# Letting the second part's experts go some 20 items into the third group's 48-point stage instead of at the end of the sort

## The chip, the cores and the metric

The kernel runs on one core of a Trainium2 chip. The metric is the device time of one execution in microseconds. Before the change it is 2397.02 us, the median of three runs (2395.26 to 2405.26).

## What is computed

A causal convolution along the sequence, by FFT in the reference, feeds a mixture of experts in which each token goes to one expert:

```python
L = 2 * S                                   # S = 5696, x: 8 x 5696 x 128
y = irfft(rfft(x, n=L) * rfft(h, n=L), n=L)[:, :S]
x = y.reshape(8 * 5696, 128)
expert_idx = argmax(x @ w_gate, axis=1)     # 8 experts
gate_w = softmax(x @ w_gate)[expert_idx]
for e in range(8):                          # w1[e]: 128 x 1024, w2[e]: 1024 x 128
    out[expert_idx == e] = gate_w * (relu(x @ w1[e]) @ w2[e])
```

## The kernel before

The eight sequences are split into three groups of 2, 3 and 3 (`SPLIT`), and each group has one part, which is the unit of sorting and of expert work. A group passes through these stages:

- `phase_a`: 119-point transforms of the input, stored to `U` in DRAM. For the third group it runs as a *guest* inside the second group's sort (class `Guest`), and its stores of `U` are at L271.
- `phase_b`: the 48-point stage. It has 120 items, one for each frequency `q`, in 30 blocks of 4. An item goes through: a cut of the input into a high and a low half (L488 on ScalarE, L490 on VectorE), three forward matmuls (L472, tile `xp`), two copies (L499, L500), a product on VectorE (L503) and one on GpSimd (L504), their sum on VectorE (L510), the inverse matmul (L518, tile `vp`), a save (L527), and a store to `V` (L563). For each block it loads `uq` from `U` (L418), `mi` (L421) and `hh` (L425) on SyncE's queue, and the forward matrices `mt` on GpSimd's queue (L407). It prefetches two blocks before its first item and further blocks two ahead.
- `phase_c`, called by `gather`: the last transform (L652), routing, and the sort. Each column of tokens is scattered to its expert's region of `SR` by an indirect DMA on GpSimd's queue (L589). What is left of them is put out at the end of `phase_c`, so all of them stand ahead of whatever GpSimd gets next. Then `tables` computes on VectorE which rows and which expert each tile of 256 tokens has, and notes the last eight scatters in `pt.ends`.
- `moe`: the experts. The second part has 67 tiles of four steps each. A step has six matmuls of layer 1 (L993), a ReLU on ScalarE (L999), its remainder on VectorE (L1001) and six matmuls of layer 2 (L1013). For each tile the rows `xr` are loaded on SyncE (L943, behind a read of the table at L941 and a wait for `pt.ends`), weights `wb` where the expert changes (L962), rows transposed on TensorE (tile `mx`), the result drained (L1023) and scattered by GpSimd (L1036).

The order of all instructions is written out by a planner, `run`, which draws on two streams, `experts()` and `rest()`. Each `yield` names a cost; a stream's clock advances by the cost over its share (1.0 for the experts, 0.75 for the rest), and the stream that is furthest behind writes its next instructions. This is the order in which every engine and every queue executes. `experts()` gives way as long as `pt.ready` of the next part is not set; when it is set, it takes the other stream's time. By these costs, the first part's 37 tiles end just as the second group's `phase_c` ends, and `rest()` goes on with the third group's `phase_b`, which yields 6000 once (`GAPS[1]`) and 998.4 for each item. The third group's `gather` follows.

Of the kernel before, what the change touches and what calls it, by code (L numbers as in the profile page):

```python
# [48 lines left out]
GAPS = (0, 6000, 5000)  # L49
HOLD = (0, 0, 0)  # L50
AHEAD = 2
A3 = (True, True, False)
ALO = ('gpsimd', 'vector', 'vector')
AT = 650
# [10 lines left out]
def conv_moe(ctx: ExitStack, tc: tile.TileContext, I, out, B, S, D, E, F, split):  # L65
# [68 lines left out]
    for g, nbs in enumerate(split):  # L134
        gr = Group(g, b0, sum(nbs))
# [104 lines left out]
    def steps_a(gr, tag, bufs):  # L240
# [7 lines left out]
        xts, uts, xss = {}, {}, {}  # L248
        split = A3[g]

# [56 lines left out]
    def phase_a(gr):  # L307
        start, begin, store, flush, M = steps_a(gr, "six", SIX)
        half = AT if gr.g == 0 else 750 * RATE[3 * gr.g - 3]
        start()  # L310
        for m in range(M + 2):
            if m < M:
                begin(m)
            yield half
            flush()
            if 1 <= m <= M:
                store(m - 1)
        yield 0
        flush()

    class Guest:
# [4 lines left out]
        def begin(self, count):  # L326
            if self.m == 0:
                self.start()
            for _ in range(min(count, self.M - self.m)):
                self.step(self.m)  # L330
                self.open.append(self.m)
                self.m += 1
# [6 lines left out]
        def rest(self):  # L339
            while self.m < self.M:  # L340
                self.begin(2)
                yield 1500 * RATE[3 * self.gr.g - 3]
                self.end()
            yield 0
            self.flush()
# [260 lines left out]
    def phase_c(pt, guest=None):  # L606
# [27 lines left out]
        def divide(n, k):  # L634
            if not pt.c3 or n >= nu:
                return
            src = vqs[n][:, :, k * cw : (k + 1) * cw]
            vr = sb.tile([QN, 2, 2, cw], F32R, tag="six", name=f"vr{g}_{n}_{k}", bufs=SIX)
            nc.scalar.copy(vr[:, 0], src)
            nc.vector.tensor_tensor(out=vr[:, 1], in0=src, in1=vr[:, 0].bitcast(F32), op=ALU.subtract)  # L640
            vrs[n, k] = vr
# [15 lines left out]
        def settle(n, k):  # L657
            if k == 0:
                rt = sb.tile([MP, NI, nb, RW], F32, tag="rt", name=f"rt{g}_{n}", bufs=6)
                nc.vector.tensor_tensor(  # L660
                    out=rt[:, :, :, D + 1].bitcast(I32),
                    in0=idb[:, pt.b0 : pt.b0 + nb].rearrange("p (o b) -> p o b", o=1).broadcast_to([MP, NI, nb]),
                    in1=ioff[:, n * NI : (n + 1) * NI].rearrange("p (i o) -> p i o", o=1).broadcast_to([MP, NI, nb]),
                    op=ALU.add,
                )
                rts[n] = rt.rearrange("p i b w -> p (i b) w")
            done = nc.scalar.copy(
                rts[n][:, k * cb : (k + 1) * cb, :D],
                ybank.pop((n, k))[:MP, :cw].rearrange("p (b d) -> p b d", d=D),
            )  # L670
            sort_one(done.ins)
# [127 lines left out]
        if gr.g:  # L799
            yield GAPS[2]  # L800
        for k in range(AHEAD):
            divide(*divmod(k, nsub))
# [4 lines left out]
        for n in range(n_end + 1):  # L807
            for k in range(nsub):
# [18 lines left out]
                if n < nu:  # L827
                    divide(*divmod(at + AHEAD, nsub))
                    settle(n, k)
# [84 lines left out]
    def fill(pt):  # L914
        g, base = pt.s, state["base"]
        dr = sb.tile([1, E], I32, tag="dr", name=f"dr{g}")
        nc.vector.tensor_copy(dr, base[0:1, :E])
        yield 20000
        for e in range(-1, E):
            row = E * CAP  # L920
            if e >= 0:
                row = nc.sync.value_load(dr[0:1, e : e + 1], min_val=0, max_val=E * CAP - T)
            s = nc.sync.dma_start(SR[ds(row, T), :].rearrange("(p s) w -> p s w", s=2), dummy).ins
            tc.declare_no_dep(s, group="sr", reason="rows past the last token of an expert")
            tc.add_to_no_dep_group("sr", s)
            pt.ends = pt.ends + [s]
            yield 2000
# [174 lines left out]
    def gather(pt, guest=None):  # L1102
        state["hold"] = HOLD[pt.s]
        yield from phase_c(pt, guest)
        state["hold"] = 0
        tables(pt)
        if pt is parts[-1]:
            yield from fill(pt)
        pt.ready = True
        yield 0  # L1110

    def chain(*gens):
# [2 lines left out]

    def rest():
        yield from phase_a(groups[1])
        for gr in groups[1:]:
            yield from phase_b(gr)
            guest = Guest(groups[gr.g + 1]) if gr.g + 1 < len(groups) else None  # L1120
            for pt in gr.parts:
                yield from gather(pt, guest)
            if guest:
                yield from guest.rest()

    def experts():
        for pt in parts:
            while not pt.ready:
                yield None
            yield from moe(pt)  # L1130
# [29 lines left out]
    with tc.manual_schedule():  # L1160
        prep = weights()
        back = rest()
        run((phase_a(g0), 1.0), (phase_h(), SHARES[4]), (consts(), 1.0), (prep, SHARES[5]), stop=(prep,))
        sb.close()
        sb.open("b")
        first = phase_b(g0)
        run((first, 1.0), (prep, SHARES[0]), until=first)
        sb.close()
        sb.close()
        sb.open("sb")  # L1170
        first = chain(*[gather(pt) for pt in g0.parts])
        run((first, 1.0), (prep, SHARES[1]), (back, SHARES[2]), until=first)
        run((prep, 1.0))
        lull = pause(LULL[0])
        run((lull, 1.0), (back, LULL[1]), until=lull)
        run((experts(), 1.0), (back, SHARES[3]))
        sb.close()
# [78 lines left out]
```

## Time and profile before

| | us |
|---|---|
| median of three runs | 2397.02 (2395.26 to 2405.26) |
| the profiled execution | 2403.89 |
| its span, first to last instruction | 2402.1 |
| mean granted TensorE clock | 0.945 |

| engine | busy us | share of the span |
|---|---|---|
| TensorE matmul (PE) | 2111.8 | 88% |
| TensorE weight load (PEld) | 1797.5 | 75% |
| VectorE (DVE) | 1599.4 | 67% |
| ScalarE (ACT) | 1453.6 | 61% |
| GpSimd (POOL) | 1236.6 | 51% |

A busy time is the union of an engine's instructions; issuing a DMA from SyncE does not count as busy, but SyncE's queue is served in order, so that an instruction that waits there holds up all behind it. The share is a mean over stages with different limits, so the stretch around the change has to be read by itself. In rows, "[38.16 <-DMA xr<-SR]" is the engine's idle time before the instruction and what ended it; "Lnnn" is a line of the kernel.

### The profile page before, as it was taken

Reading aid. Unit: us, or ns where it says so; the run is one execution under the profiler, and the core shown is the slowest. Engines: PE = TensorE matmul, PEld = TensorE weight load, DVE = VectorE, ACT = ScalarE, POOL = GpSimd, SP = SyncE. Lnnn points to the kernel's source line nnn. Section 1 sums busy time; section 2 is a strip of 40 time slices with the busy share of each in tenths; the row PEclk is TensorE's granted clock in tenths of the full one; section 3 lists DMA queues with packets and bytes.
Section 4 is the critical chain, followed back from the end, with each engine's and each line's share of the span. In section 5 each row is a group of like instructions: output and inputs, shape, how many; then the busy total and the mean of one; then the engine's idle time right before and its main releaser. Section 6 shows DMA issues by size and latency. Waiting matters only on the chain.

```text
span 2402.1 us, 48507 instructions
## 1 busy us (share of the span) xinstructions
PE 2111.8 (88%) x14238; PEld 1797.5 (75%) x14238; DVE 1599.4 (67%) x3807; ACT 1453.6 (61%) x3193; POOL 1236.6 (51%) x1281
## 2 busy tenths in 40 slices
PE   6888687659898899995689988999987899999998
PEld 4666454437677777774678777899877899999998
DVE  3578654559898746665599998767665455555554
ACT  3699653348888745552588887666543444444444
POOL 4487536725555427677355555457776223232323
PEclk8999898769999999997899999999998999999999
DMA  8999898699999678883898998566633222222221
GB/s 250 307 280 297 249 317 232 195 247 239 234 261 235 170 203 248 250 251 103 193 224 205 228 209 209 137 157 172 164 87 100 81 77 80 75 77 77 79 75 34
DMA packets 274473, 439.10 MB, mean 183 GB/s; under 512 B 32433, under 2 KB 200679, under 8 KB 274208
## 3 DMA queue, kind: packets, MB, share of 16 engines
q1 hardware_dynamic: 243552, 365.29, 56.7%
q0 software_dynamic: 30656, 70.69, 10.6%
q8 instruction: 116, 1.90, 0.3%
q14 instruction: 149, 1.22, 0.2%
HBM read 601.91 MB, written 166.06 MB: 320 GB/s over the span
## 4 chain that ended last, share of the span: by engine, by line
PE 48%; DMA 17%; issue 12%; DVE 7%; ACT 7%; POOL 4%; SPq 3%; POOLq 0%; DVEq 0%; ACTq 0%
PE mh L993 14%; PE ma L1013 14%; PE yp L652 5%; PE pa L278 4%; DMA wb<-WD 4%; DMA SR<-rt,pi 3%; DMA xt<-x 2%; PE vp L518 2%; PE mx L166 2%; DVE hs L1001 2%; DMA mi<-miq 2%; POOL out L1036 2%; PE tp L691 2%; PE xp L472 1%; ACT xs L500 1%
## 5 line engine op out<-in xcount | busy, mean ns | idle before, releaser
L993 PE MATMUL mh<-xtb,wb 128*128 128x256 f32 x4368 | 726.6, 302 | 79.5 <-DVE hs L1001 47.4
L1001 DVE SCALAR_TENSOR_TENSOR hs<-mh,hs 128x512 fp32r<-128x512 f32 x728 | 499.7, 686 | 411.4 <-ACT hs L999 410.9
L993 PEld LDWEIGHTS mh<-xtb,wb 128*128 128x128 f32 x4368 | 594.4, 192 | 184.4 <-DVE hs L1001 77.9
L999 ACT ACTIVATE hs<-mh 128x512 fp32r<-128x512 f32 x728 | 435.2, 598 | 460.8 <-PE mh L993 458.2
L1036 POOL DMA_INDIRECT out<-xr x364 | 369.8, 1016 | 638.0 <-DVE xr L1027 557.2
L1013 PE MATMUL ma<-hs,wb 128*128 128x256 f32 x4368 | 661.8, 288 | 10.0 <-DMA wb<-WD 9.8
L1013 PEld LDWEIGHTS ma<-hs,wb 128*128 128x128 f32 x4368 | 578.6, 192 | 13.8 <-DMA wb<-WD 13.1
L589 POOL DMA_INDIRECT SR<-rt,pi x384 | 394.0, 1026 | 214.4 <-issue 73.6
L504 POOL TENSOR_TENSOR xs<-xs,hh 128x384 f32<-128x384 f32 (+1 forms) x360 | 345.4, 971 | 255.9 <-ACT xs L500 221.9
L510 DVE TENSOR_TENSOR zt<-zt,xs 128x384 f32<-128x384 f32 (+1 forms) x300 | 293.0, 977 | 44.2 <-POOL xs L504 44.2
L518 PE MATMUL vp<-zt,mi 128*96 128x384 f32 (+1 forms) x720 | 274.7, 464 | 17.9 <-DVE vt L527 9.3
L472 PE MATMUL xp<-us,mt 96*128 96x384 f32 x720 | 193.4, 374 | 28.6 <-DVE us L490 14.5
L503 DVE TENSOR_TENSOR zt<-xp,hh 128x384 f32<-128x384 f32 (+1 forms) x360 | 180.8, 502 | 40.8 <-ACT xs L500 39.7
L499 ACT ACTIVATE xs<-xp 64x384 f32<-64x384 f32 (+1 forms) x360 | 162.8, 452 | 36.2 <-DVE zt L510 24.2
L488 ACT CAST us<-uq 96x384 fp32r<-96x384 f32 x240 | 123.2, 514 | 75.5 <-PE xp L472 57.2
L472 PEld LDWEIGHTS xp<-us,mt 96*128 96x128 f32 x720 | 124.6, 199 | 57.1 <-DVE us L490 24.8
L490 DVE TENSOR_TENSOR us<-uq,us 96x384 fp32r<-96x384 f32 x240 | 149.7, 625 | 22.9 <-ACT us L488 22.7
L500 ACT COPY xs<-xp 64x384 f32<-64x384 f32 (+1 forms) x360 | 156.6, 435 | 4.2
L518 PEld LDWEIGHTS vp<-zt,mi 128*96 128x96 f32 x720 | 111.9, 166 | 55.2 <-POOL xs L504 25.3
L278 PE MATMUL pa<-xc,fcr 120*120 120x512 f32 x360 | 115.1, 461 | 35.0 <-ACT ut L290 12.5
L527 ACT COPY vt<-vp 96x384 f32<-96x384 f32 x240 | 114.1, 476 | 11.2 <-PE vp L518 5.5
L278 PEld LDWEIGHTS pa<-xc,fcr 120*120 120x120 f32 x360 | 71.3, 212 | 62.9 <-ACT xc L256 13.5
(129 smaller groups left out, 2592.2 us busy)
## 6 DMA issues: line engine op xcount, KB each, us to landing
wb<-WD SPq DMA_DIRECT2D x728, 512.0 KB
vq<-V SPq DMA_DIRECT2D x64, 720.0 KB
U<-ut SPq DMA_DIRECT2D x48, 720.0 KB
uq<-U SPq DMA_DIRECT2D x60, 576.0 KB
V<-vt SPq DMA_DIRECT2D x60, 576.0 KB
xr<-SR SPq DMA_DIRECT2D x182, 130.0 KB
xt<-x SPq DMA_DIRECT2D x96, 240.0 KB
mt<-mqs POOLq DMA_DIRECT2D x60, 384.0 KB
```

The lines of the kernel that those rows point to most:

```text
L278: nc.tensor.matmul(banks[m][:QN, :], lhs, rhs, start=(k == 0), stop=(k == len(ops) - 1))
L472: nc.tensor.matmul(xp[:, :cw], mt[:, at + u, :], us[:, v], start=(k == 0), stop=(k == 2))
L503: nc.vector.tensor_tensor(out=zt, in0=x3, in1=hv[:, 0].broadcast_to([P, cb, D]), op=ALU.mult)
L504: nc.gpsimd.tensor_tensor(out=xs, in0=xs, in1=hv[:, 1].broadcast_to([P, cb, D]), op=ALU.mult)
L510: eng.tensor_tensor(out=zt, in0=zt, in1=xs, op=ALU.add)
L518: nc.tensor.matmul(vp[:K2, :cw], mi[:, k0, :], zt.rearrange("p b d -> p (b d)"), start=True, stop=True)
L589: s = nc.gpsimd.indirect_dma_start(out=SR[:, :], out_offset=IndirectOffsetOnAxis(ap=pi[:, b : b + 1], axis=0), in_=rt[:, b, :], in_offset= ...
L993: nc.tensor.matmul(hp[:, u, :], wb[:, a, f, :], xt[:, b, :], start=(n == 0), stop=(n == 2))
L999: done = nc.scalar.activation(hs[:, 0], hp, AF.Relu)
L1001: nc.vector.scalar_tensor_tensor(out=hs[:, 1], in0=hp, scalar=0.0, in1=hs[:, 0].bitcast(F32), op0=ALU.max, op1=ALU.subtract)
L1013: nc.tensor.matmul(accs[j], wb[:, a, f, :], hs[:, b, u, :], start=(k == 0 and u == 0 and n == 0), stop=(k == NPAIR - 1 and u == 1 and n == 2),
L1036: sc = nc.gpsimd.indirect_dma_start(out=out[:, :], out_offset=IndirectOffsetOnAxis(ap=xr[:, s, D + 1 : D + 2].bitcast(I32), axis=0), in_=x ...
```

## The change

A part whose sort has a guest is no longer marked ready at the end of its sort. `rest()` keeps it in a list and marks it ready when the next group's `phase_b` has spent more than `HEAD` of the planner's cost. Only the second part has a guest, so only its experts are concerned.

```diff
+HEAD = 26000
@@ gather
         if pt is parts[-1]:
             yield from fill(pt)
-        pt.ready = True
+        if guest is None:
+            pt.ready = True
         yield 0
@@ rest
         yield from phase_a(groups[1])
+        wait = []
         for gr in groups[1:]:
-            yield from phase_b(gr)
+            spent = 0
+            for cost in phase_b(gr):
+                spent += cost
+                yield cost
+                if spent > HEAD and wait:
+                    wait.pop().ready = True
             guest = Guest(groups[gr.g + 1]) if gr.g + 1 < len(groups) else None
             for pt in gr.parts:
                 yield from gather(pt, guest)
             if guest:
                 yield from guest.rest()
+                wait.append(gr.parts[-1])
```

## Rows read from the trace of the kernel before

**Rows 1.** The page's span in 40 slices: TensorE's busy tenths in each

```profile
PE   6888687659898899995689988999987899999998
```

**Rows 2.** Stretches: length, busy us (instructions) by engine, granted clock, DMA share, GB/s

```profile
core 0: us, PE busy (x) PEld busy (x) DVE busy (x) ACT busy (x) POOL busy (x), PEclk, DMA share, GB/s
1120.00:1140.00 20.00, 0.00 (x0) 0.00 (x0) 5.90 (x18) 0.00 (x0) 15.27 (x16) 0.50 0.17 48
1140.00:1160.00 20.00, 5.60 (x25) 4.97 (x26) 1.81 (x3) 1.86 (x4) 5.28 (x7) 0.51 0.83 229
...
1940.00:2380.00 440.00, 435.23 (x3633) 431.80 (x3632) 239.26 (x420) 211.24 (x420) 135.00 (x139) 1.00 0.25 75
```

**Rows 3.** Waits of SyncE's queue, 1085 to 1185: total us, times, longest us

```profile
SPq L943 <- DMA SR<-rt,pi: 20.6, 3, 17.8
SPq L941 <- DVE ej L895: 19.3, 1, 19.3
```

**Rows 4.** Timeline of GpSimd: start, us, line, operation, tiles, count, idle before

```profile
1143.59 0.99 POOL L589 DMA_INDIRECT SR<-rt,pi  x1 [0.31 <-issue]
1144.59 1.62 POOL L407 DMA_DIRECT2D mt<-mqs  x3
```

**Rows 5.** Timeline of SyncE's DMA issues in the same stretch

```profile
1101.86 3.89 SPq L271 DMA_DIRECT2D U<-ut  x2
1146.44 2.69 SPq L943 DMA_DIRECT2D xr<-SR  x3
1150.26 2.26 SPq L962 DMA_DIRECT2D wb<-WD  x4
...
1153.70 0.43 SPq L418 DMA_DIRECT2D uq<-U  x1
```

**Rows 6.** Timeline of TensorE: first expert matmuls, first item, item 22 (1233.09)

```profile
1153.07 0.66 PE L166 MATMUL mx_None<-ident,xr 128*128 128x128 f32 x2 [38.16 <-DMA xr<-SR]
1154.93 4.68 PE L993 MATMUL mh<-xtb,wb 128*128 128x256 f32 x18 [1.20 <-DMA wb<-WD]
...
1169.65 0.79 PE L472 MATMUL xp<-us,mt 96*128 96x384 f32 x3
...
1233.09 0.69 PE L472 MATMUL xp<-us,mt 96*128 96x384 f32 x3
```

**Rows 7.** Line 993 from 1154 to 1233.1: count, ns min/median/max, first and last start

```profile
L993 PE MATMUL mh<-xtb,wb x162: 277/282/582, 1154.9 to 1231.8; 128*128 128x256 f32 x162
```

**Rows 8.** Timeline at the second group's first items: SyncE and TensorE

```profile
477.32 10.73 SPq L271 DMA_DIRECT2D U<-ut  x4
513.58 2.67 SPq L943 DMA_DIRECT2D xr<-SR  x3
500.11 4.42 PE L472 MATMUL xp<-us,mt 96*128 96x384 f32 x10 [13.13 <-ACT us L488]
...
522.18 0.69 PE L166 MATMUL mx_None<-ident,xr 128*128 128x128 f32 x2 [5.50 <-DMA xr<-SR]
525.96 1.62 PE L993 MATMUL mh<-xtb,wb 128*128 128x256 f32 x6 [3.09 <-DMA wb<-WD]
```

**Rows 9.** Line 472 from 500 to 516

```profile
L472 PE MATMUL xp<-us,mt x27: 338/525/1095, 500.1 to 515.6; 96*128 96x384 f32 x27
```

**Rows 10.** VectorE's groups, 505 to 516: count, busy us, mean ns, idle before

```profile
L510 DVE TENSOR_TENSOR zt<-zt,xs 128x384 f32<-128x384 f32 x6 | 5.5, 910 | 0.0
L490 DVE TENSOR_TENSOR us<-uq,us 96x384 fp32r<-96x384 f32 x5 | 4.6, 915 | 0.0
L503 DVE TENSOR_TENSOR zt<-xp,hh 128x384 f32<-128x384 f32 x6 | 3.3, 545 | 0.1
```

**Rows 11.** Line 1023, one drain a tile, from 1940 to 2380

```profile
L1023 ACT COPY ot<-ma x70: 372/373/374, 1940.9 to 2375.9; 128x256 f32<-128x256 f32 x70
```

**Rows 12.** Waits of the engines, 1775 to 1850

```profile
DVE pi L784 <- DMA SR<-rt,pi: 6.6, 1, 6.6
```

**Rows 13.** Stretch after the restart in the second group's stage

```profile
525.00:530.00 5.00, 4.04 (x13) 3.37 (x14) 1.72 (x3) 1.57 (x4) 0.75 (x1) 0.50 1.03 401
```

## The prediction

> **What bounds the kernel now.** I read the page's forty slices first [rows 1]. TensorE is at 0.8 to 0.9 almost everywhere, with one hole in the nineteenth and twentieth slice, 1081 to 1201 us. The table of stretches [rows 2] places it: TensorE does nothing from 1120 to 1140, 5.60 us of work from 1140 to 1160, and in the last stretch, where only experts are left, 435.23 of 440 us. So the end is set by TensorE with expert tiles, and whatever is put off to the end is paid there at TensorE's full price.
>
> SyncE's waits tell what it did in the hole [rows 3]: its first instructions for the second part's experts stood 19.3 us for the table (L941) and 17.8 us at most for the sort's scatters (L943). The same wait is seen from GpSimd [rows 4]: the scatters (L589) go out one by one until 1143.59 + 0.99 us, and only behind them the third group's matrices `mt` (L407) at 1144.59. On SyncE [rows 5] the last store of `U` starts in the run at 1101.86, then nothing until the rows `xr` at 1146.44, the weights `wb` at 1150.26, and the third group's first `uq` at 1153.70, behind the experts. On TensorE [rows 6] the row transposes come at 1153.07 after 38.16 us idle, the first expert matmul at 1154.93, the first matmul of the 48-point stage (L472) at 1169.65.
>
> **What the change moves, by the code.** `HEAD` is 26000. `phase_b` of the third group yields 6000 once, then 0.78 x 384 x 8 / 2.4 = 998.4 an item; 6000 + 21 x 998.4 = 26966 is the first sum above it, and that resumption also writes out the next item. So 22 items (0 to 21) stand ahead of the second part's first expert instruction on every queue; before, the experts stood ahead of item 0. No instruction is added or removed, and no wait.
> - SyncE: the table reads, 3 `xr` and 4 `wb` loads move behind the loads of blocks 0 to 6 and the `V` stores of blocks 0 to 3. The last of these waits for item 15's save, so SyncE comes to the experts when TensorE is at about item 21.
> - GpSimd: nothing is moved past the scatters; `mt` still follows them. The experts' output scatters of the first tiles go later, onto a queue that is free then; I price that at nothing. Cover gone, it would be two instructions a tile of about 1 us each.
> - TensorE, VectorE, ScalarE: the first expert steps move behind 22 items. Their number is counted: when item 22's first matmul ran in the profile, at 1233.09 us [rows 6], 162 matmuls of layer 1 had started [rows 7], six to a step, 27 steps. After the change one step stands there. So 26 steps, 6.5 tiles, are put off.
>
> **The sum.** I compare the moment at which item 22 runs, since from there the interleaving is the same in both (0.75 against 1), and then add the 6.5 tiles that are still owed.
> 1. Start of the stage. `uq` can go as soon as `U` has landed and no longer waits for the experts, but the first matmul also needs `mt`, issued at 1144.59. How long `mt` takes to land isn't shown; the weights, 512 KB, went from issue to first use in 4.7 us (1150.26 to 1154.93), `mt` is 384 KB: I take 4.4, so 1149. Ends: 1147 and 1151. Of the hole, only its last 5 us are filled.
> 2. Items 0 to 21 alone. The profile has the same situation once: the second group's stage ran its first items alone just before the first part's experts [rows 8, 9]. Ten matmuls, over three items, took 4.42 us, so 1.4 us an item while the pipeline fills; 27 matmuls, nine items, started from 500.1 to 515.6. Steady, VectorE is full: 910 + 915 + 545 = 2370 ns an item [rows 10]. I take 4 x 1.4 + 17 x 2.3 = 44.7 us from item 0's start to item 21's, so 1193.7. Ends: (515.6 - 500.1) / 9 = 1.7 for all 21 (36 us), and the mixed pace (1233.09 - 1169.65) / 22 = 2.9 for the 17 (55 us).
> 3. The experts' start in mid-stage. TensorE takes its queue in order: the row transposes wait for `xr`, and the items behind them wait too. From SyncE's first `xr` to the first expert matmul it was 8.5 us in the hole (1146.44 to 1154.93) and 12.4 us in the earlier case (513.58 to 525.96, with 5.50 us idle ahead of the transposes and 3.09 for `wb`) [rows 8]. I take 11, as the earlier case has the same loads in flight: 1204.7. Item 22 follows its step by 1.4: 1206.1.
> 4. After that wait the granted clock was 0.50 for the 5 us after restart [rows 13]; that costs 2 us here (ends 0 and 5): 1208.1.
> So item 22 runs 1233.1 - 1208.1 = 25.0 us earlier. The 6.5 tiles owed run at the end among experts alone: 70 drains from 1940.9 to 2375.9 are 435.0 / 69 = 6.30 us a tile [rows 11], 41.0 us (at a tile per 7.6 us, as behind the second sort, it would be 49). Net 41.0 - 25.0 = **16 us slower**.
>
> The reason in a sentence: in the mixed stage TensorE works on experts while VectorE works on items, and the change takes 6.5 tiles out of that mixture, though the hole they were meant to leave is held open by GpSimd's queue.
>
> The second sort's end is also a weak place: VectorE waits 6.6 us for a scatter (L784) [rows 12]. After the change 18.5 instead of 12 tiles of the second part remain there by the planner's costs, but TensorE stood behind VectorE's queue, not without tiles; I price it at nothing, ends -4 and +4.
>
> The profiled execution took 2403.89 us (span 2402.1), 6.9 above the median of the runs, 2397.02. The sum gives 2419.9 for an execution like the profiled one, and 2413 for the median.
>
> **Rivals.**
> - *Faster: the items fill the hole.* Place: the first L472 matmul. If `mt` did not wait behind the scatters, item 0 would need only `uq`. Earlier it ran 12.1 us after the last `U` store's issue ended (477.32 + 10.73 = 488.05 to 500.11) [rows 8]; from 1101.86 + 3.89 = 1105.75 that gives 1118. Then item 22 runs at 1118 + 59.1 = 1177, 56 us earlier, net -15: 2382. It decides once the first matmul is ahead of 1233 - 41 - 59 = 1133. For it: SyncE is free from 1106. Against: `mt` came right behind the last scatter, and the diff changes nothing ahead of it on GpSimd. Chance 0.07. The Trainium skill speaks for this rival: its page "DMA: Bandwidth & Descriptors", section "Issuing engines are not separate DMA queues", says that transfers issued from different engines interleave on the same sixteen engines and that the issuing engine matters only for the sequencer's time, usually small. By that the wait on GpSimd would be minor and 2382 would come out; the row shows over 30 us of issuing ahead of `mt`, so I hold to the row.
> - *The experts' start is hidden.* If SyncE runs so far ahead that `xr` and `wb` are there when TensorE arrives, steps 3 and 4 cost nothing: item 22 at 1193.7 + 1.4 = 1195.1, 38 us earlier, net +3: 2400. For: SyncE prefetches three blocks. Against: it passes a `V` store that waits for item 15. Chance 0.13.
> - *The hold does nothing that counts,* because the tiles put off find idle TensorE time later (the 0.9 of the mixed stage, the second sort's end): net about 0, 2397. For: TensorE isn't full there. Against: the planner keeps the same ratio of experts to items. Chance 0.06.
>
> **How the numbers follow.** The forecast has 0.74; with its ends (item 22 at 1195 or at 1225, 6.30 to 7.6 us a tile) it spans about +2 to +36 us, and its lower fifth, 0.14, lies within 12 us of no change. A measurement of this kernel can tell about 0.5%, 12 us, from no change. Slower by more: 0.60. Within: 0.14 + 0.13 + 0.06 = 0.33. Faster: 0.07. The range 2398 to 2430 takes in the forecast but its outermost end, and the hidden start; it leaves out the first rival and about half of the third.
>
> **What would show it.** Right: first L472 matmul of the third group at 1147 to 1151, behind the last scatter and `mt`; about 2.3 us from item to item; then a gap of 5 to 9 us on TensorE at the row transposes; item 22 at about 1208; the second part's first expert matmul at about 1205 instead of 1154.93; tail tiles at 6.3 us and the last tile 16 us later. Wrong: an L472 matmul ahead of 1133; items alone at under 1.8 us; no gap at the transposes; or a mixed stage after item 22 whose pace differs from before.

## The result, and the profile after

The changed kernel took 2426.97 us (median of seven runs, 2421.22 to 2434.33); the kernel before, in seven runs beside them, 2397.02 (2393.15 to 2410.83). The ratio is 1.0126, with a 95% interval of 1.0104 to 1.0148: 30 us slower, where the forecast was 16 in a range of 1 to 33. The profiled execution of after took 2434.33 us (span 2432.5), 30.4 us of span more than the profiled one of before.

The slices and stretches of after, read as [rows 1, 2] (the first line is the page's row of slices; the others give length, busy time of each engine with its instructions, granted clock, DMA share, GB/s):

```profile
PE   7888697568998799993798898999968999999998
1120.00:1140.00 20.00, 0.00 (x0) 0.00 (x0) 6.73 (x20) 0.00 (x0) 15.42 (x16) 0.50 0.74 178
1140.00:1160.00 20.00, 9.66 (x23) 6.29 (x23) 8.34 (x12) 8.41 (x18) 10.96 (x13) 0.50 0.37 81
1160.00:1190.00 30.00, 24.07 (x72) 11.99 (x71) 30.00 (x43) 26.39 (x56) 16.97 (x17) 0.91 0.98 214
1940.00:2380.00 440.00, 433.44 (x3592) 429.70 (x3592) 236.46 (x414) 208.97 (x415) 134.24 (x139) 0.99 0.25 75
```

TensorE's hole from 1120 to 1140 is there as before, and the stage of experts alone is as full as before. In the stretch in which items now run alone, 1160 to 1190, it is VectorE that is busy for 30.00 of 30.00 us. The slices have a new dent, the "6" in the thirtieth, 1764 to 1824 us, where the third group's sort ends.

The start of the stage in the timelines of after (SyncE's issues, GpSimd, TensorE), the answer to [rows 4 to 6]:

```profile
1105.27 0.33 SPq L272 DMA_DIRECT2D U<-ut  x1
1110.50 0.33 SPq L419 DMA_DIRECT2D uq<-U  x1
1193.14 2.98 SPq L944 DMA_DIRECT2D xr<-SR  x3
...
1143.49 1.00 POOL L590 DMA_INDIRECT SR<-rt,pi  x1 [0.30 <-issue]
1144.47 1.65 POOL L408 DMA_DIRECT2D mt<-mqs  x3
...
1149.34 4.12 PE L473 MATMUL xp<-us,mt 96*128 96x384 f32 x10 [34.47 <-DMA mt<-mqs]
1198.75 0.69 PE L167 MATMUL mx_None<-ident,xr 128*128 128x128 f32 x2 [4.31 <-DMA xr<-SR]
1200.68 1.62 PE L994 MATMUL mh<-xtb,wb 128*128 128x256 f32 x6 [1.24 <-DMA wb<-WD]
1202.10 1.16 PE L473 MATMUL xp<-us,mt 96*128 96x384 f32 x3
```

SyncE fetched the first `uq` at 1110.50, 43 us earlier than before, but the first matmul of the stage stands at 1149.34 and names `mt`, which GpSimd issued right behind the last scatter. The experts follow at 1200.68, item 22 at 1202.10.

To see where the time went, I set marks in both traces: the time at which the same work runs, and how many of the second part's tiles had started by then (matmuls of layer 1 over 24). "First sort" and "second sort" are those of the second and the third group. The marks come from groups by line, before and after (count, ns min/median/max, first and last start): layer 1 up to the second sort's first matmul, the inverse matmuls, the second sort's transform (`yp`) and its gate matmuls (`tp`).

```profile
L993 PE MATMUL mh<-xtb,wb x780: 277/281/988, 1154.9 to 1549.2; 128*128 128x256 f32 x195
L994 PE MATMUL mh<-xtb,wb x630: 277/281/988, 1200.7 to 1524.8; 128*128 128x256 f32 x158
...
L518 PE MATMUL vp<-zt,mi x240: 483/486/847, 1178.5 to 1535.9; 128*96 128x384 f32 x120
L519 PE MATMUL vp<-zt,mi x240: 483/486/927, 1156.6 to 1500.4; 128*96 128x384 f32 x120
L652 PE MATMUL yp<-vr,gcr x288: 335/337/434, 1550.2 to 1776.8; 120*120 120x384 f32 x144
L653 PE MATMUL yp<-vr,gcr x288: 335/337/343, 1525.6 to 1753.5; 120*120 120x384 f32 x144
L691 PE MATMUL tp<-yt,c_moe_w_gate x288: 265/278/291, 1559.7 to 1784.7; 128*32 128x120 f32 x144
L692 PE MATMUL tp<-yt,c_moe_w_gate x288: 266/278/291, 1534.2 to 1761.4; 128*32 128x120 f32 x144
```

| mark | before, at tile | after, at tile | after earlier by |
|---|---|---|---|
| item 22, first matmul | 1233.1, 6.75 | 1202.1, 0.25 | 31.0 |
| last inverse matmul (`vp`) of the 48-point stage | 1535.9, 30.25 | 1500.4, 24 | 35.5 |
| first matmul of the second sort (`yp`) | 1550.2, 32.5 | 1525.6, 26.25 | 24.5 |
| last gate matmul (`tp`) of the second sort | 1784.7, 54 | 1761.4, 47.75 | 23.3 |
| first matmul of layer 1 behind the second part's 67 tiles ("tile 67") | 1900.8, 67 | 1925.8, 67 | -25.0 |
| end of the span | 2402.1 | 2432.5 | -30.4 |

Beside the tiles that are owed, the loss shows in three places. At the seam between the 48-point stage and the second sort, the lead of 35.5 becomes 24.5: **11 us**. From the last gate matmul to tile 67 there were 13 tiles in 116.1 us and now 19.25 in 164.4: 48.3 us more for 6.25 tiles, which at 6.30 us are 39.4, so **8.9 us** too many. And 5.4 us go behind tile 67, mostly at one wait for weights (2.77 us at 2330.56), which a second profile of this kernel (the run e4 below) doesn't repeat.

The marks add up: 39.4 owed, 11.0, 8.9 and 5.4, and 1.2 inside the sort, less the 31.0 of item 22 and the 4.5 won from there to the seam, are the 30.4 us of span. The 4.5 is mostly a matter of this one profile of before: it took 302.8 us from item 22 to the last `vp`, a second one (e5 below) 299.0, and after 298.3.

The 11 us in the trace of after: SyncE's issues at that seam, the waits of TensorE, and the stretch of the second wait (columns as above).

```profile
1504.78 0.80 SPq L963 DMA_DIRECT2D wb<-WD  x2
1505.69 1.83 SPq L622 DMA_DIRECT2D vq<-V  x2
1507.88 1.06 SPq L963 DMA_DIRECT2D wb<-WD  x2
...
1508.66 0.95 PE L994 MATMUL mh<-xtb,wb 128*128 128x256 f32 x6 [1.59 <-DMA wb<-WD]
1518.18 1.62 PE L994 MATMUL mh<-xtb,wb 128*128 128x256 f32 x6 [6.43 <-DMA wb<-WD]
...
1514.00:1524.00 10.00, 5.82 (x27) 5.85 (x28) 1.50 (x4) 1.72 (x4) 1.57 (x2) 0.50 0.58 199
```

Weights are loaded only where the expert changes, four loads of 512 KB for the tile. With 6.5 tiles less behind it, the part's third change of expert, its fourth load of weights, now moves its 2 MB at 1505 to 1520, on the same queue and at the same time as the first `vq` loads of the sort (720 KB each). TensorE waits 1.59 and 6.43 us for the weights, and the granted clock is 0.50, 1.2 of 2.4 GHz, for the ten microseconds from 1514, 2.2 us into the second wait. Before, that change fell at 1462 to 1481, still inside the 48-point stage.

### The profile page after: what moved, and what is told of

Read it like the earlier page. It is cut to its first block, busy times and chain, and to the rows that moved or that the text cites. A ratio compares the mean times of both kernels' runs of the same rounds, so it can differ in the third digit from the quotient of the medians.

```text
span 2432.5 us, 48539 instructions
## 1 busy us (share of the span) xinstructions
PE 2123.6 (87%) x14238; PEld 1795.5 (74%) x14238; DVE 1606.3 (66%) x3807; ACT 1456.0 (60%) x3193; POOL 1239.0 (51%) x1281
## 4 chain that ended last, share of the span: by engine, by line
PE 31%; DMA 8%; issue 7%; POOL 3%; DVE 2%; ACT 1%; SPq 1%; POOLq 0%; DVEq 0%; ACTq 0%
PE mh L994 12%; PE ma L1014 12%; DMA wb<-WD 3%; DMA SR<-rt,pi 2%; PE mx L167 2%; PE yp L653 2%; POOL out L1037 1%; PE xp L473 1%; DMA mi<-miq 1%; PE vp L519 1%; POOL xs L505 1%; DVE hs L1002 1%; DMA mt<-mqs 1%; PE tp L167 1%; PE tp L692 1%
## 5 line engine op out<-in xcount | busy, mean ns | idle before, releaser
L1014 PEld LDWEIGHTS ma<-hs,wb 128*128 128x128 f32 x4368 | 577.8, 192 | 21.4 <-DMA wb<-WD 20.8
L590 POOL DMA_INDIRECT SR<-rt,pi x384 | 399.8, 1041 | 212.8 <-issue 68.9
L511 DVE TENSOR_TENSOR zt<-zt,xs 128x384 f32<-128x384 f32 (+1 forms) x300 | 286.1, 954 | 40.2 <-POOL xs L505 40.2
L473 PE MATMUL xp<-us,mt 96*128 96x384 f32 x720 | 207.4, 390 | 74.8 <-DMA mt<-mqs 34.5
L504 DVE TENSOR_TENSOR zt<-xp,hh 128x384 f32<-128x384 f32 (+1 forms) x360 | 180.8, 502 | 37.9 <-ACT xs L501 36.9
L491 DVE TENSOR_TENSOR us<-uq,us 96x384 fp32r<-96x384 f32 x240 | 161.7, 675 | 45.8 <-ACT us L489 45.7
L500 ACT ACTIVATE xs<-xp 64x384 f32<-64x384 f32 (+1 forms) x360 | 162.7, 452 | 37.5 <-DVE zt L511 26.5
L279 PE MATMUL pa<-xc,fcr 120*120 120x512 f32 x360 | 110.8, 447 | 36.3 <-ACT xc L257 13.4
L653 PE MATMUL yp<-vr,gcr 120*120 120x384 f32 x576 | 116.5, 337 | 0.9 <-DVE vr L641 0.6
```

What stands on the lines that cost most here:

```text
L473: nc.tensor.matmul(xp[:, :cw], mt[:, at + u, :], us[:, v], start=(k == 0), stop=(k == 2))
L504: nc.vector.tensor_tensor(out=zt, in0=x3, in1=hv[:, 0].broadcast_to([P, cb, D]), op=ALU.mult)
L511: eng.tensor_tensor(out=zt, in0=zt, in1=xs, op=ALU.add)
L590: s = nc.gpsimd.indirect_dma_start(out=SR[:, :], out_offset=IndirectOffsetOnAxis(ap=pi[:, b : b + 1], axis=0), in_=rt[:, b, :], in_offset= ...
L653: nc.tensor.matmul(yp[:MP, :cw], lhs, rhs, start=(m == 0), stop=(m == len(ops) - 1))
L1014: nc.tensor.matmul(accs[j], wb[:, a, f, :], hs[:, b, u, :], start=(k == 0 and u == 0 and n == 0), stop=(k == NPAIR - 1 and u == 1 and n == 2),
```

## The experiments

Where e1 to e4 and f1 to f4 ran, the sorts are slower (before took 2538 and 2543 us there; e4's second sort takes 302 us from its first `yp` to its last gate matmul, before's 235), so each run is compared with before on its own device, and a ratio below is of that.

### GpSimd's queue, and what stands in it

**e1.** The matrices of the first two blocks go out ahead of the last eighteen scatters, all else as after:

```diff
@@ phase_c, where the last guest step is written
+                if guest and n == nu + 1 and k == 0:
+                    for qb in range(EARLY):                  # 2
+                        ahead[2, qb] = matrices(2, 4 * qb)   # the dma_start of mt
@@ phase_b
-            if cutting:
+            if (g, qb) in ahead:
+                mt = ahead.pop((g, qb))
+            elif cutting:
```

> The changed kernel, with the matrices mt of the third group's blocks 0 and 1 issued on GpSimd ahead of the last 18 scatters instead of behind them. If mt alone holds the stage back, the first matmul of the third group's stage (1149.3 us after the change) comes at about 1123, all 22 items run some 26 us earlier and the time falls by about 26 us, to 2401. If GpSimd's queue holds the stage as a whole, the items' product on GpSimd still waits behind the scatters: the first forward matmuls come at about 1123, they stop after three to six items, the stage goes on at about 1146, item 22 runs some 4 to 9 us earlier than at 1202.1, and the time is about 2420.

Measured: 1.0053 (1.0025 to 1.0082) of before. TensorE's and GpSimd's timelines of e1 (start, length, line, tiles, count, idle before):

```profile
1181.88 0.66 PE L482 MATMUL xp<-us,mt 96*128 96x384 f32 x1 [7.05 <-DMA mt<-mqs]
1186.48 5.35 PE L482 MATMUL xp<-us,mt 96*128 96x384 f32 x12 [3.94 <-DVE us L500]
1208.55 1.01 PE L482 MATMUL xp<-us,mt 96*128 96x384 f32 x2 [16.71 <-DVE us L500]
...
1203.25 1.00 POOL L599 DMA_INDIRECT SR<-rt,pi  x1 [0.30 <-issue]
1204.83 3.24 POOL L514 TENSOR_TENSOR xs<-xs,hh 128x384 f32<-128x384 f32 x3
```

The first item runs 21 us ahead of the last scatter, so `mt` did hold the start. But only 13 forward matmuls get in, four items and a third of the next; then the stage stands for 16.71 us, because the product that each item needs on GpSimd (L514 here) stands behind the scatters too. Item 22 is 49.3 us behind the last scatter instead of 59.8 in e4, 10.5 us earlier. So what holds the stage is the whole queue of GpSimd, not one load in it. The time, 13 us over before, lies between what was expected for the two cases (4 and 23 us); it is the trace that decides for the second.

**e2.** So the products of the first eight items go to VectorE as well, and the experts are let go after eight items:

```diff
-HEAD = 26000
+HEAD = 12500
-            nc.gpsimd.tensor_tensor(out=xs, in0=xs, in1=hv[:, 1].broadcast_to([P, cb, D]), op=ALU.mult)
+            eng = nc.vector if g == 2 and n < FIRST else nc.gpsimd      # FIRST = 8
+            eng.tensor_tensor(out=xs, in0=xs, in1=hv[:, 1].broadcast_to([P, cb, D]), op=ALU.mult)
```

> As the last one, and besides the products of items 0 to 7 on VectorE instead of GpSimd, and HEAD 12500, so that 8 items stand ahead of the second part's experts. If GpSimd's queue is what keeps the hole open, the stage starts at about 1123, the 8 items are done by about 1145, and the first expert matmul comes at about 1155 as before the change. Item 8 then runs at about 1157 instead of 1190.5 before, 33 us earlier, and 12 steps, 3 tiles, are owed at 6.3 us, 19 us: about 2383, 14 us faster than before the change. If the hole has another cause (SyncE's loads, the landing of U), the start stays near 1149 and the time is about 2405.

Measured: 0.999 (0.996 to 1.0021), no change: a miss. **e8** goes further: e2 without the wait of the plan between sort and stage.

```diff
-GAPS = (0, 6000, 5000)
+GAPS = (0, 0, 5000)
-HEAD = 12500
+HEAD = 6500
```

> mt of blocks 0 and 1 ahead of the last 18 scatters, products of items 0 to 7 on VectorE, and no GAPS cost ahead of item 0, with HEAD 6500, so that 8 items stand ahead of the second part's experts. The hole takes the 8 items, and of the 12 steps that were owed with the GAPS cost only about 6.5 remain, 1.6 tiles or 10 us. If the owed tiles at 6.3 us each are what is lost, it is 5 to 9 us faster than the run with HEAD 12500 and the GAPS cost, 0.4% to 0.9% faster than before. If they are not, it equals that run, within 0.2% of before.

Measured: 0.9997 (0.9985 to 1.0009): no gain, the second of the two cases. Yet the hole was filled. TensorE in e8:

```profile
1118.19 4.12 PE L483 MATMUL xp<-us,mt 96*128 96x384 f32 x10 [13.25 <-DMA mt<-mqs]
...
1130.78 0.86 PE L530 MATMUL vp<-zt,mi 128*96 128x384 f32 x2
1148.70 0.69 PE L169 MATMUL mx_None<-ident,xr 128*128 128x128 f32 x2 [17.06 <-DMA xr<-SR]
1150.80 1.62 PE L1008 MATMUL mh<-xtb,wb 128*128 128x256 f32 x6 [1.42 <-DMA wb<-WD]
```

Item 0 runs at 1118.19. That the prediction's first rival named 1118 is chance: it counted 12.1 us from the last store of `U`, which in e8 ends at 1095.8, and here item 0 waited for `mt`, issued at 1108.58. The forward matmuls of eight items have run by 1131.6, and then TensorE stands 17.06 us at the row transposes, for which the sort's last scatters must be through. Against the run e5 (before again, on the same device), counted from the last scatter, item 22 comes 36.6 us earlier (51.4 against 88.0), with 3 tiles owed (18.9 us): on paper 17.7 us gained. Of these, 3.4 are gone because the last scatter itself is later (1140.0 against 1136.6), 3.0 up to the second sort's last gate matmul (lead on the span's clock 33.2, then 30.2), and 8.3 behind it: to tile 67 the sixteen tiles take 143.8 us against e5's thirteen in 116.6, 27.2 more for 18.9 owed. Tile 67 starts 3 us earlier, and the time is the same.

**e3, f3.** The other direction: one item ahead of the experts (`HEAD = 0`), and that without the plan's wait.

```diff
-HEAD = 26000
+HEAD = 0
```

> The changed kernel with HEAD 0: one item instead of 22 stands ahead of the second part's experts, with the loads of its first blocks. If the loss is the expert tiles that are put off, only 7 steps (1.6 tiles, 10 us) are owed here, the items gain about 13 us, and the time is about 2394. If holding the experts back costs something that doesn't grow with the number of items (the restart, the order on SyncE), most of the 30 us stay: about 2420.

```diff
-HEAD = 26000
+HEAD = 0
-GAPS = (0, 6000, 5000)
+GAPS = (0, 0, 5000)
```

> The changed kernel with HEAD 0 and no GAPS cost ahead of the third group's first item: two items and the loads of the first blocks stand ahead of the second part's experts, and 1 step is owed (2 us). If expert tiles put off are what is lost and the loads ahead of the experts are a gain, it is 10 to 14 us faster than before. If the gain seen with HEAD 0 (0.4%) came from the experts' steps that the GAPS cost lets stand alone, it is no faster than before.

Measured: e3 0.9959 (0.9925 to 0.9993), about 10 us faster than before, where 3 were expected; f3 0.9952 (0.9925 to 0.998), about 12. One item ahead is therefore a small gain and not a loss, as 22 are. Counted from the last scatter, e3's item 22 comes at 72.6 us, where before has 89.5 and e5 88.0, with 1.5 tiles (9.5 us) owed. The plan's wait adds nothing that can be told from e3.

### The change of expert at the seam

**e4, e5.** After and before once more, unchanged, for a second profile of each.

> The changed kernel once more, for a second profile. What belongs to the order of instructions comes again at the same place: a wait of about 8 us for weights where the 48-point stage meets the second sort (1505 to 1520), about 9 us more than before the change around the sort's end (1760 to 1865). The wait for weights at 2330, 2.8 us and a clock of one half behind it, 5 us in all, comes again if it is of that kind and is gone if it is chance.

> The kernel before, for a profile from the same chip as the next three. From the last inverse matmul of the third group's 48-point stage to the first matmul of the second sort's stage it should again be about 14 us for 2.25 tiles (1535.9 to 1550.2), with no wait for weights there.

Measured: e4 1.0109 (1.0052 to 1.0166), e5 0.9995 (0.9976 to 1.0014). The wait at 2330 has no counterpart in e4, whose stretch behind tile 67 takes 504.4 us (after 506.7, before 501.3, e5 502.3). TensorE's wait at the seam is there again in e4:

```profile
1567.47 1.62 PE L994 MATMUL mh<-xtb,wb 128*128 128x256 f32 x6 [6.83 <-DMA wb<-WD]
```

From the last `vp` to the first `yp`, 2.25 tiles in each of the two, before took 14.3 us and e5 14.1, both without a wait for weights; after took 25.2 and e4 24.3.

**e6, e7.** Before and after with no loading of weights at a change of expert: only the first expert of each part is loaded. These two leave out the weights of all the others, so they tell the price of the loads, as waits and as traffic.

```diff
-        nc.vector.tensor_tensor(out=tab[:, 2, 1:], in0=ej[:, 1:], in1=ej[:, : NT - 1], op=ALU.not_equal)
+        nc.vector.tensor_tensor(out=tab[:, 2, 1:], in0=ej[:, 1:], in1=ej[:, 1:], op=ALU.not_equal)
```

> The kernel before, in which only the first tile of each part loads weights and the other seven experts' weights of that part are left out. Fewer weights are read, 7 x 2 MB less in each of three parts; by the waits for weights in the profile of before (2.6 and 1.6 us at the fourth change of expert, 2.8 us and less elsewhere) it should be 5 to 15 us faster than before.

> The changed kernel with the same part left out. If the loss beyond the expert tiles put off (41 us owed, 31 us earlier, 10 us net) comes from changes of expert that now fall on the seam of the stages and on the sort's end, the distance to the kernel before without changes of expert shrinks from 30 us to 10 to 15 us, and the seam takes about 14 us as before. If the loss lies in the order of the queues whatever is loaded, the distance stays at 25 to 30 us.

Measured: e6 0.9947 (0.9927 to 0.9968), 2380.64 us; e7 0.9998 (0.9982 to 1.0014), 2391.04. Their distance is 10.4 us (by the ends of the two intervals 3 to 21) where before and after differ by 30. The seam in e7, TensorE's last `vp` and first `yp`:

```profile
1490.54 0.81 PE L519 MATMUL vp<-zt,mi 128*96 128x384 f32 x2
1504.96 1.56 PE L653 MATMUL yp<-vr,gcr 120*120 120x384 f32 x6
```

From the last of the two matmuls of that `vp` group, at 1490.9, to `yp` it is 14.1 us, and in e6 14.2: what before takes, against 25.2 in after. So it is the loads that make the 11 us. Set side by side step for step, after and e7 run alike to 0.1 us from tile 23 to 24.75 and from 26.5 to 28, and after loses 10.75 us between them. That the sort's first `vq` loads are the other half of it is argued and not tested by a run: the DMA engines are full (busy share 1.02) from 1512 to 1518 while TensorE waits, but in before the next change of expert, at 1562 to 1577 between later `vq` loads, holds TensorE up nowhere. At the seam the experts also run alone, 2.25 tiles in 14 us.

From the first sort's last scatter to the end of the span e6 took 1244.5 us and e7 1254.8, 10.3 more. By the sum it would be the 41.0 owed less the lead of item 22, which from the last scatter is 29.7 in this pair: 11.3.

### More room for rows

**f1, f2, f4.** At the second sort's end SyncE waited for a free row buffer, 4.6 us before and 11.8 after, by its waits before (1770 to 1850) and after (1755 to 1870):

```profile
SPq L943 <- DMA out<-xr: 4.6, 1, 4.6
```

```profile
SPq L944 <- DMA out<-xr: 11.8, 1, 11.8
```

Behind such a wait stand the loads of `wb`, which each tile issues and which move something only where the expert changes. TensorE waited there later, by its timeline of after:

```profile
1813.48 1.62 PE L994 MATMUL mh<-xtb,wb 128*128 128x256 f32 x6 [8.56 <-DMA wb<-WD]
```

So eight row buffers instead of seven, with two buffers of the sort given up for the room: f1 is after with it, f2 before, f4 e8.

```diff
-XR = 7
+XR = 8
-            t = sb.tile([32 * cb, MP], F32, tag="lt", name=f"lt{g}_{n}_{k}", bufs=6)
+            t = sb.tile([32 * cb, MP], F32, tag="lt", name=f"lt{g}_{n}_{k}", bufs=4)
```

> The changed kernel with 8 instead of 7 row buffers (XR; the logits' buffers lt go from 6 to 4 for the room). At the second sort's end SyncE waited 11.8 us for a row buffer whose output scatter stood behind the sort's scatters, and TensorE then 8.56 us for weights (1813.5). If the row buffers are what costs there, one more buffer, a tile's time, takes most of that wait away, and the distance to the kernel before with the same edit is some 7 us smaller than 30 us. If the wait only covers another (VectorE's or GpSimd's queue), the distance stays at about 30 us.

> The kernel before with the same edit, as the base of the last one. SyncE's wait for a row buffer there was 4.6 us and TensorE's waits for weights behind it 1.0 to 1.5 us a tile, so it should be within 5 us of before; fewer lt buffers alone could make it slower in the sort.

> The run that fills the hole with 8 items, with 8 row buffers. That run equalled before although item 22 was some 37 us earlier and only 3 tiles, 19 us, were owed; 8 us were lost at the second sort's end, with a wait for weights of 7.39 us behind SyncE's wait for row buffers. If the row buffers are the cause, this one is 6 to 9 us faster than before with the same edit. If not, it equals it.

Measured: f1 1.0014 (0.9994 to 1.0035), 2549.42 us; f2 0.9949 (0.9926 to 0.9973), 2529.62; f4 0.9861 (0.9824 to 0.9897), 2509.43 against 2543.46. Before gains 0.5%, 14 us, by this edit, more than the 5 expected, and the distance of after to it is 19.8 us instead of 30; e4's interval, 13 to 42 us on its device, doesn't tell that from no change of the distance. The seam in f1 still has its 24.7 us (f2 14.0). From the last gate matmul to tile 67 f1 takes 163.5 us and e4, with seven buffers, 164.9: the eighth buffer is worth 1.4 us there. Behind tile 67, where no sort runs, these two profiles differ by more, 497.4 us against 504.4.

The wait for a row buffer isn't what makes most of the 8.9 us at the second sort's end. e7 tells it: SyncE waits for a row buffer there and TensorE behind it, as in after, though no weights are moved (SyncE's waits from 1720 to 1850, TensorE's timeline):

```profile
SPq L944 <- DMA out<-xr: 12.8, 1, 12.8
...
1790.43 1.62 PE L994 MATMUL mh<-xtb,wb 128*128 128x256 f32 x6 [9.57 <-DMA wb<-WD]
```

Yet e7 loses only 2.1 us at the sort's end. So a wait put down to `wb` can be one for SyncE to come past a load that moves nothing; in after no weights moved from 1793 to 1851 either. Step for step, after is 0.5 us behind e7 from the last gate matmul to tile 56.75 and 6.1 at tile 58.25: what it loses beyond e7 goes, but for 1.1 at tile 67, at the change of expert that moves its weights at 1852 to 1863.

f4 beats both kernels, by 1.4% on before and by 0.8% on f2 (2509.43 against 2529.62), more than either case expected. Why it gains where e8 did not is not settled: its profiled execution, 2529.90 us, is the longest of its six, so the trace doesn't show the gain; where it ran, SyncE waited for no row buffer there even in e4, so that f1 and f4 could not test that wait; e8 and f4 were not run on one device, and the smaller `lt` was not tried alone.

## Why the prediction was right, and where its size came from

**The direction and its reason held.** The hole stays open, as forecast, and the cause is the one named, GpSimd's queue, more than the load named in it (e1). The Trainium skill's page "DMA: Bandwidth & Descriptors", section "Issuing engines are not separate DMA queues", says that starting DMAs from several engines only saves sequencer time, usually small beside the DMA itself. Here it was not small: over 30 us of scatters stood ahead of `mt` (1112 to 1144), and moving the load up started the stage 21.4 us ahead of the last scatter (e1) instead of 6.0 behind it (e4).

**The steps.**
1. Start of the stage: forecast 1149, measured 1149.34.
2. Items alone: forecast 44.7 us for 21 items. Measured 42.5, by the group of after up to item 21's first matmul, the 64th (count, ns min/median/max, first and last start), and VectorE's groups from 1155 to 1190 (count, busy us, mean ns, idle before):

```profile
L473 PE MATMUL xp<-us,mt x64: 332/522/1095, 1149.3 to 1191.8; 96*128 96x384 f32 x64
...
L491 DVE TENSOR_TENSOR us<-uq,us 96x384 fp32r<-96x384 f32 x17 | 17.3, 1019 | 0.0
L511 DVE TENSOR_TENSOR zt<-zt,xs 128x384 f32<-128x384 f32 x17 | 14.3, 839 | 0.0
L504 DVE TENSOR_TENSOR zt<-xp,hh 128x384 f32<-128x384 f32 x16 | 8.7, 543 | 0.0
```

   VectorE is the bound of the items alone, as forecast: it is busy for 30.00 of 30 us. But the sum of the three means, 1019 + 839 + 543 = 2401 ns here and 2370 in [rows 10], isn't the pace. The records overlap (17.3 + 14.3 + 8.7 = 40.3 us in a stretch of 35, and 13.4 in the 11 us of [rows 10]); from item 8 to item 21 it was 1163.68 to 1191.76, 2.16 us an item.

3. The experts' start: forecast 11 us from SyncE's first `xr` to the first expert matmul, ends 8.5 and 12.4. Measured 1200.68 - 1193.14 = 7.5, below the lower end. The mistake was to call the earlier case of [rows 8] the nearer one. The wait at the transposes is there, 4.31 us, though shorter than the 5 to 9 foretold.
4. The clock after the wait: 2 us in the sum. The clock was there (0.50 from 1198 to 1206), but item 22 follows its step by 1200.68 to 1202.10, the 1.4 us of the sum, so nothing of the 2 us is in this lead.

So item 22 is 31.0 us earlier instead of 25.0: of the 6.0 us, 2.2 come from step 2, 3.5 from step 3, 2 from step 4, and 1.6 go the other way, since SyncE comes to `xr` 1.3 behind item 21's first matmul and the start is 0.3 later. The 26 steps owed are exact (6.75 against 0.25 tiles), and the price at the end too:

```profile
L1024 ACT COPY ot<-ma x59: 372/373/374, 1941.9 to 2307.5; 128x256 f32<-128x256 f32 x59
```

This is (2307.5 - 1941.9) / 58 = 6.30 us a tile, as in [rows 11]. By its own steps the sum should have come out at 10, and without the loads at a change of expert it does: e7 less e6 is 10.4 us.

**What failed** are the places that the sum priced at nothing.
- The seam between stage and sort had no term at all: 11 us. I counted the tiles that were put off but not which tile then meets which stage. The tile that changes expert brings 2 MB, and it came to stand on the seam. e4 repeats the loss, and e7 shows that it needs these loads.
- The second sort's end was priced at nothing with ends of 4: it took 8.9. I had looked for idle tiles or VectorE there. In e7 the same stretch is only 2.1 us over 6.30 a tile (157.2 us for 19.25 tiles against e6's 115.8 for 13), so 6.8 of it need the loads too, mostly at one change of expert. Why that change costs more in after than in before isn't shown.
- The last 5.4 us come mostly at a wait that e4 doesn't repeat, and no step of mine stands for them.

So 10 by the mechanism and 11 and 9 by the two places make the 30; what else differs between the two profiles (4.5 won ahead of the seam, 5.4 lost at the end) nearly cancels. That the time lies in the range, 30 in 1 to 33, is in part luck: by its own mechanism the forecast should have been 10, and a lead taken 6 us too short stood in for losses that it didn't know.

**The rivals.** "The experts' start is hidden" didn't happen: SyncE came to `xr` 1.3 us behind item 21. "The hold does nothing that counts" is excluded by the ratio's interval. "Faster" was excluded for the reason given, but its price was wrong twice: with `mt` early, the product on GpSimd still holds the stage (e1), and with both out of the way (e8), the net is nothing rather than -15, although e8 keeps only eight items ahead.

## What to carry to other kernels

When work is put off, count not only how much but which pieces then meet which stage: a piece with a load of its own (here the 2 MB of a new expert) that slid onto the seam of two stages cost 11 us, as much as the 10 by which the work put off outweighed the lead. A stage starts when the last of all queues that its first item passes is free, so move the head of each before expecting a hole to fill. And a gain that is measured at one mark need not reach the end: e8 had 17.7 us in hand at item 22 and none at the end.

## What was not expected of the hardware

A single wait of 6.43 us on TensorE came with ten microseconds at half clock. Ahead of it the engine was busy for 10.16 of 14 us at a granted clock of 0.99; the clock stood at 0.50 from 1514 to 1524, so that the matmuls behind the wait ran at half speed as well (six of layer 1 in 1.62 us, and in 0.88 at 1524.22).

VectorE's instructions with both inputs in SBUF, 96 to 128 partitions by 384, took 839 to 1019 ns on average in the stage alone, while the product with an input from `xp`, in PSUM, took 543. The difference goes with GpSimd: in the whole trace of after, the 164 subtractions L491 during which no GpSimd product ran took 537 to 555 ns, and the 76 that ran beside one took 960 on average. The product L504 took at most 559 ns, beside one or not.
